# First layer in 512-token tiles for the last 1536 tokens, with a new opening list: a fused attention and two-MLP kernel

## The chip, the cores and the metric

One core of a Trainium2 chip runs the whole kernel. The metric is the device time of one execution in microseconds (us); three runs give a median. TensorE does the matmuls, VectorE (DVE in the rows), ScalarE (ACT) and GpSimd (POOL) the elementwise work, and SyncE (SP) issues most transfers.

## The reference

A banded attention (each token sees the 64 tokens up to itself) over 4 sequences of 576 tokens, 8 heads of 64, then two MLPs, the first with a leaky Relu whose slope is given by column, the second with x times sigmoid(x):

```python
scores = scale * np.matmul(q, k.transpose(0, 1, 3, 2))
mask = (rel >= 0) & (rel < window)              # rel = row - column, window = 64
scores = np.where(mask, scores, -1000000000.0)
attn = np.exp(scores - np.max(scores, axis=-1, keepdims=True))
attn = attn / (np.sum(attn, axis=-1, keepdims=True) + 1e-09)
x = np.matmul(attn, v)                          # laid out as 2304 tokens x 512
...
h = x @ w_in                                    # 512 -> 2048
g = np.maximum(h, 0.0) + alpha * np.minimum(h, 0.0)
x = g @ w_out                                   # 2048 -> 512
...
h = x @ w_in2
out = (h * (1.0 / (1.0 + np.exp(-h)))) @ w_out2
```

All is float32. Where more precision than one pass is wanted the kernel writes a number as a high and a low part and adds three products (high by high, high by low, low by high).

## The kernel before, in words

The 2304 tokens lie in six tiles of 384 (`TN`). An **item** is one tile and one pair of heads, so there are 24; items 0 to 3 make tile 0. An item goes through scores (`mm_s`, S in the list, line 220), the row maximum (`peaks`, m, L231, VectorE), the exponential (`exps`, e, L243, ScalarE), the sum's reciprocal (`over`, r), the scaling (`scaled`, s: on GpSimd with P, on ScalarE with A at L267, else on VectorE), transposes (`mm_t`, t, L278), a copy out of PSUM (`keep_t`, k, L287), the product with v (`mm_v`, P, L300), and the split of the result into a high part (`high_v`, x, L310, ScalarE) and a low part (`low_v`, l, L316, VectorE). m, e, r, s, t and k go by halves a and b.

The first layer's product `mlp_h1` (M, L400) takes, for one tile and one of 16 blocks of 128 columns (f), 4 x 3 matmuls into a bank h. `fall_g1` (G, L406, ScalarE) and `join_g1` (J, L415, VectorE) make the leaky Relu, and `store_g1` (L428) writes it to device memory.

The program has these stages. **The opening**: a list written out by hand, `START`, gives the order of items 0 to 11, of the scores and softmax of 12 and 13, of the conversion of the 16 weight blocks (c, h, o), and of all first-layer work of tiles 0 and 1. **The rest of the first layer**: a loop over tiles 2 to 5 and f, 64 steps; every eighth step begins a group with two more items (`begin`), and a plan of numbered places (`hook`) puts the conversion of later weights between the steps. **The first layer's second product** (L496): 3 x 56 steps of Strassen-like sums with parts named A11, A21, A22, A12; `load_g1` (L445) fetches the Relu's results, `sum_g1` (L453) adds, `split_g1` splits into high and low parts (L346, L347), three steps ahead of their use. Then the second MLP (L575, L695 and L699).

Small tiles have fixed places: `room(i)` in one pool, `wroom(i)` in another, both by hand. Each engine works through its own queue in order; a wait holds all behind it.

Of the kernel before, what the change touches and what calls it, by code (L numbers as in the profile page):

```python
# [20 lines left out]
q0 q2 S0 S2 m0a q3 S3 m0b m2a z m2b q1 e0a e0b e2a r0b S1 v0 q5 q4 e2b r0aP s0aP r2a m3a m3b r2b m1a t0a m1b s2aP e3a  # L21
e3b t2a r3aP S5 k2aD k0aD s2bP e1a e1b s0bP s3aP S4 m5a e5a m5b r1aP r3bP q7 r1bP t2b q6 v1 v2 q8 m4a t0b k2bD S7 S6
s1aP s1bP k0bD e4a m7a t1a e5b t3a t1b s3bP m4b r5aP m6a r4aP t3b r5bP m6b e4b P0 s5aP k3b P2 k1aD k1bD s5bP t5a e6a
k3aD t5b r4bP m7b P1 e6b k5aD s4aP s4bP P3 x2 r6b t4b e7a l2 t4a S8 v5 v6 r6aP v4 w1 k5bD s6bP k4bD r7aP t6b k4a m8a
e7b x0 x3 m8b r7b s6aP q9 q11 P4 P5 k6b s7aP s7bP q10 t6a c1a l0 l3 t7a e8a k7a c1b t7b x1 w6 S9 k7bD k6a P7 P6 x4 c1c
h1 x7 l1 x5 e8b r8aP m9a m9b s8aP e9a l7 w7 S11 S10 o1 l5 l4 r8b t8a s8bA M0.1.1 M1.1.3 c6a m10a M0.1.2 r9aP x6 v8 v9
M0.1.3 M1.1.0 e9b t8b k8b c6b s9aP w2 M1.1.1 k8aD l6 w3 q13 r9b c6c M0.1.0 m10b P8 c7a h6 c7b e10a t9a s9bP v10 t9b
k9b o6D m11a k9a M1.1.2 M0.6.1 M1.6.0 c7c m11b e11a G1.1 c2a h7 c3a x8 M0.6.2 M0.6.0 r10aP c3b r11a l8 e10b M1.6.2 c2b
e11b o7D M1.6.1 M1.6.3 r11b s10aP c3c P9 G0.1 w8 w5 q12 x9 t10a M0.6.3 M1.7.2 M0.7.0 k10a M0.7.2 G1.6 h3 l9 r10bP
M1.7.3 M1.7.1 M0.7.3 c2c v11 s11aA J0.1 J1.1 G0.6 s10bA M1.7.0 s11bA J1.6 J0.6 o3 M0.7.1 t10b t11a t11b c8a k10b c8b  # L30
P10 c5a c5b k11a k11b S12 S13 c5c c8c h5 m12a G1.7 P11 M1.3.2 h8 m13a h2 o5 m12b m13b x11 J1.7 o2D w10 w4 w9 x10 c10a
o8 l11 c10b M0.5.3 M1.3.3 M0.8.3 M1.8.2 M1.2.0 l10 c4a c10c M1.2.2 M0.2.1 c4b M1.3.0 c4c M1.2.3 G0.7 M1.5.0 h10 M1.5.3
M1.8.1 M1.5.1 h4 w11 o10D o4 M1.5.2 M1.3.1 M0.8.2 M1.2.1 c11a c11b G1.5 G1.3 c11c c9a M0.2.2 M0.8.1 M1.8.0 J1.3 J1.5
h11 M0.8.0 w12 w0 w13 c9b M1.10.1 c12a c0a c9c M0.10.1 M0.2.3 G1.2 G0.8 c12b M1.10.3 M1.10.0 M0.5.0 J0.8 c12c M0.5.2
M0.2.0 G0.2 M0.4.1 M0.4.2 M0.10.2 h9 c0b M1.10.2 J0.7 J0.2 o11D o9 h12 M0.5.1 M0.11.0 M0.11.2 w14 v12 v13 w15 e12a
J1.2 o12 c13a M0.11.1 e12b M1.12.1 M0.4.0 c14a M0.4.3 c0c M0.3.3 M1.8.3 c13b M0.11.3 c13c M1.12.2 c15a M1.12.3 G0.5
M0.10.3 G0.4 G1.8 G0.11 J0.5 M1.9.0 c15b c15c M1.9.3 M0.10.0 M1.9.1 M0.3.2 h15 J0.4 G0.10 M1.11.3 M1.11.1 J1.8 J0.10
M1.9.2 G1.9 M0.12.0 h0 h13 M1.4.0 M0.12.1 c14b M1.12.0 o15D o0D M0.3.0 M1.11.2 M1.4.2 M0.3.1 M0.12.3 c14c M1.11.0 o13
J1.9 M0.15.0 h14 M0.12.2 J0.11 G1.12 J1.12 o14 r12a M0.15.1 G0.3 M0.0.3 J0.3 G1.10 M1.14.0 M0.0.1 M1.14.3 M0.0.0
M0.15.2 e13a G1.11 M0.15.3 M1.14.2 M0.9.3 J1.10 M1.14.1 M1.13.2 J1.11 M1.4.1 M1.0.1 G0.12 G0.15 M1.13.3 M1.13.1 J0.12  # L40
M0.14.1 M1.0.2 e13b M0.14.0 M0.9.1 M1.13.0 s12aP r13bP M0.0.2 M1.4.3 G0.0 r13a r12bP M1.0.3 M0.14.3 M1.0.0 J0.15 G1.4
M0.9.0 M0.9.2 M0.14.2 M0.13.1 G1.14 G1.13 s13bA s12bA J1.13 M0.13.3 G1.0 G0.14 G0.9 M0.13.0 M0.13.2 J0.9 J1.4 J1.14
G0.13 M1.15.3 J0.0 J0.14 M1.15.1 J0.13 M1.15.0 J1.0 M1.15.2 s13aP G1.15 J1.15
# [8 lines left out]
def attention_two_mlps(ctx, tc, q, k, v, w_in1, w_out1, alpha, w_in2, w_out2, out):  # L52
# [7 lines left out]
    TN = 384  # L60
    NTILE = NT // TN
# [24 lines left out]

    def room(i, shape=None, dtype=F32, name="r"):
        return rp.tile(shape or [P, TN], dtype, name=name, tag=f"r{i}")

# [50 lines left out]
    AHEAD = 3 * NHP  # L140
    spare = {"pr": [*range(28, 34), 36, 37], "pt": [38, 39, 34, 35], "bank": list(range(8))}
# [4 lines left out]
    def give(kind, i, n=0):  # L146

        if kind == "pt" and i < 36 and n == NHP + 3:
            kind = "pr"
        if kind != "pr" or i > 33 or n < NHP:  # L150
            spare[kind].append(i)
# [11 lines left out]
    def load_qk(n):  # L163
# [5 lines left out]
        queue = nc.scalar if len(items) < 3 else nc.sync  # L169
        items.setdefault(n, {}).update(qT=qt, kT=kt)  # L170
        if n == 0:
# [132 lines left out]

    def high_v(n):
        t, hp = divmod(n, NHP)

        at = 2 * hp + (32 if t == 2 else 8 * (t % 2))
        xh, xl = (wroom(at + i, [P, TN], F32R, "x") if t == 2 else room(at + i, None, F32R, "x") for i in range(2))
        nc.scalar.copy(xh, items[n]["pv"][:, :TN])  # L310
        xt[t, hp] = (xh, xl)

    def low_v(n):
        it = items.pop(n)
        xh, xl = xt[divmod(n, NHP)]
        nc.vector.tensor_tensor(out=xl, in0=it["pv"][:, :TN], in1=xh.bitcast(F32), op=ALU.subtract)  # L316
        give("bank", it["pvi"])
        if n >= AHEAD:
            load_v(n + 2)
# [67 lines left out]
    gd1 = {}  # L387
    turn_g = Turn(range(16, 28))
# [14 lines left out]
    def fall_g1(t, f):  # L403

        a = room(turn_g(), name="a")
# [5 lines left out]
    def join_g1(t, f):  # L411
# [6 lines left out]
        store_g1(3)  # L418
# [4 lines left out]
    def store_g1(keep):  # L423

        while len(unstored) > keep:
            t, f, g = unstored.pop(0)
            d = gd1[t, f] = dram.tile([P, TN], F32, name=f"g1_{t}_{f}")
# [383 lines left out]
    for w in START.split():  # L811
# [15 lines left out]
        else:  # L827
            n = int(w.rstrip("abADP"))
# [8 lines left out]
            elif x == "r":  # L837
                over(n, (hf,), engine)
# [168 lines left out]
    g = -62  # L1007
    for x in "0 1 a 2 3 b 4 5 c 6 7 d e".split():
# [36 lines left out]
    spare["pt"] += [26, 27]  # L1045
# [27 lines left out]
    for t in range(2, NTILE):  # L1073
        for f in range(KF):
            rests()
            s = (t - 2) * KF + f
            if s in group:
                begin(s, group[s])
            for x in soft.pop(s, ()):
                x()  # L1080
            mlp_h1(t, f, at=(turn_h5 if t == NTILE - 1 else turn_h)())
            fall_g1(t, f)
            if last:
                join_g1(*last)
            last = t, f
            hook((t - NTILE) * KF + f)
            if t == NTILE - 1:
                if f == 0:
                    nc.scalar.activation(out=silu_tables, in_=ident[:, :1], func=AF.Silu)
                if 4 <= f < 4 + KH:  # L1090
                    load_g1(0, A11, f - 4)
                if 8 <= f < 12:
                    load_g1(0, A21, f - 8)
                if f >= KF - 3:
                    split_g1(f - KF + 3)
# [102 lines left out]
```

## Time and profile before

| | |
|---|---|
| median of three runs | 796.95 us (796.12 to 797.12) |
| the profiled execution's own time | 795.78 us |
| its span | 794.0 us |
| TensorE busy | 784.9 us, 99% of the span |
| VectorE busy | 634.8 us, 80% |
| ScalarE busy | 491.7 us, 62% |
| GpSimd busy | 122.4 us, 15% |

The span is what the profiler saw of the program; the execution's own time holds 1.8 us more. Matmuls are pipelined, so two that follow each other overlap in the rows, and the distance of their starts is the cost of one.

### The profile page before, as it was taken

What the parts mean: (1) busy time and instruction counts of PE and PEld (TensorE: products, weight loads), DVE (VectorE), ACT (ScalarE), POOL (GpSimd) and SP (SyncE); (2) the same over time, 40 slices, a digit from 0 to 9 for tenths busy, and PEclk for the clock granted to TensorE, in tenths of its full rate; (3) what the DMA queues carried; (4) which work ended last, traced back from release to release, by engine and by line L of the source; (5) the groups of instructions that cost most, each with busy time, mean ns of one, the idle gap of its engine ahead of it and who ended that gap; (6) DMA issues with size and microseconds to landing.
All of it is one profiled execution on the core that took longest, in us unless ns stands there. A gap on an engine that the chain in (4) does not pass through costs nothing.

```text
span 794.0 us, 16666 instructions
## 1 busy us (share of the span) xinstructions
PE 784.9 (99%) x5475; PEld 754.0 (95%) x5475; DVE 634.8 (80%) x1613; ACT 491.7 (62%) x1312; POOL 122.4 (15%) x160
## 2 busy tenths in 40 slices
PE   7999999999999999999999999999999999999998
PEld 5899999999999999999999999999999888888887
DVE  6999457888888998978889775765985988868876
ACT  7974366677633675564587566545766675555553
POOL 6522200000000132231222000000000331321410
PEclk9999999999999999999999999999999999999999
DMA  9978376888595879998987765795758997958922
GB/s 298 313 254 279 124 234 219 283 258 297 186 308 207 280 154 260 285 229 237 291 238 202 241 210 184 243 335 181 247 179 274 298 263 219 209 129 235 204 50 72
DMA packets 126151, 182.79 MB, mean 230 GB/s; under 512 B 12976, under 2 KB 112048, under 8 KB 126064
## 3 DMA queue, kind: packets, MB, share of 16 engines
q1 hardware_dynamic: 111664, 162.25, 61.5%
q0 software_dynamic: 13824, 18.88, 14.5%
q8 instruction: 43, 0.70, 0.4%
q10 hardware_dynamic: 576, 0.59, 0.2%
q14 instruction: 44, 0.36, 0.1%
HBM read 105.52 MB, written 57.28 MB: 205 GB/s over the span
## 4 chain that ended last, share of the span: by engine, by line
PE 96%; ACT 1%; DVE 1%; DMA 1%; issue 0%; POOL 0%; ACTq 0%; POOLq 0%
PE h L400 25%; PE acc L496 22%; PE acc L695 15%; PE qa L575 13%; PE acc L699 7%; PE qd L575 6%; PE qb L575 3%; PE pa L300 2%; PE pa L220 2%; PE pa L278 1%; ACT pr L243 1%; DVE pr L231 1%; DMA kT<-in_k_dram 1%; PE acc L691 0%; ACT x L310 0%
## 5 line engine op out<-in xcount | busy, mean ns | idle before, releaser
L400 PE MATMUL h<-x,i 128*128 128x384 f32 x1152 | 203.1, 335 | 0.1
L400 PEld LDWEIGHTS h<-x,i 128*128 128x128 f32 x1152 | 199.0, 188 | 1.3 <-DVE i L372 0.4
L695 PE MATMUL acc<-w,gh 128*128 128x512 f32 x489 | 169.2, 394 | 0.0
L496 PE MATMUL acc<-gh,o 128*128 128x384 f32 x672 | 143.5, 334 | 0.0
L699 PE MATMUL acc<-w,gl 128*128 128x256 f32 x489 | 134.3, 277 | 0.0
L346 ACT CAST gh<-gf 128x384 fp32r<-128x384 f32 x168 | 86.2, 515 | 58.8 <-PE acc L496 52.7
L496 PEld LDWEIGHTS acc<-gh,o 128*128 128x128 f32 x672 | 118.9, 188 | 0.0
L695 PEld LDWEIGHTS acc<-w,gh 128*128 128x128 f32 x489 | 91.1, 188 | 20.6
L575 PE MATMUL qa<-v,w 128*128 128x384 f32 x576 | 107.9, 334 | 0.0
L347 DVE TENSOR_TENSOR gl<-gf,gh 128x384 fp32r<-128x384 f32 x168 | 91.5, 551 | 18.6 <-ACT gh L346 13.6
L575 PEld LDWEIGHTS qa<-v,w 128*128 128x128 f32 x576 | 100.6, 188 | 0.0
L346 ACT CAST gh<-g 128x384 fp32r<-128x384 f32 x124 | 63.6, 514 | 54.6 <-PE acc L695 48.7
L699 PEld LDWEIGHTS acc<-w,gl 128*128 128x128 f32 x489 | 91.8, 188 | 0.8
L406 ACT ACTIVATE a<-h 128x384 f32<-128x384 f32 x96 | 46.1, 489 | 72.0 <-PE h L400 69.8
L455 POOL DMA_DIRECT2D gf<-gf x48 | 42.6, 941 | 287.5 <-DVE gf L453 208.0
L496 PE MATMUL acc<-gl,o 128*128 128x384 f32 x336 | 85.2, 334 | 0.0
L347 DVE TENSOR_TENSOR gl<-g,gh 128x384 fp32r<-128x384 f32 x124 | 67.0, 552 | 13.7 <-ACT gh L346 13.3
L654 POOL DMA_DIRECT2D g<-g x40 | 34.8, 879 | 278.6 <-ACT gh L346 195.6
L415 DVE SCALAR_TENSOR_TENSOR a<-a,nalpha,h 128x384 f32<-128x384 f32 x96 | 57.0, 606 | 12.5 <-ACT a L406 12.4
L243 ACT ACTIVATE pr<-pr,nm 128x128 f32<-128x128 f32 x144 | 56.1, 394 | 10.5 <-DVE nm L231 10.4
L496 PEld LDWEIGHTS acc<-gl,o 128*128 128x128 f32 x336 | 60.7, 188 | 0.0
L575 PE MATMUL qd<-v,w 128*128 128x384 f32 x288 | 57.6, 334 | 0.0
(103 smaller groups left out, 1114.3 us busy)
## 6 DMA issues: line engine op xcount, KB each, us to landing
g<-a SPq DMA_DIRECT2D x96, 192.0 KB, 4.1
gf<-g SPq DMA_DIRECT2D x96, 192.0 KB, 4.1
g<-c SPq DMA_DIRECT2D x96, 192.0 KB, 3.3
g<-g SPq DMA_DIRECT2D x96, 192.0 KB, 4.2
s<-in_moe_w_in_dram SPq DMA_DIRECT2D x32, 512.0 KB, 5.7
s<-in_moe_w_out_dram SPq DMA_DIRECT2D x32, 512.0 KB, 5.3
gf<-gf POOLq DMA_DIRECT2D x48, 192.0 KB, 5.1
g<-g POOLq DMA_DIRECT2D x40, 192.0 KB, 4.2
```

The source lines that it names most:

```text
L243: nc.scalar.activation(out=pr[:, j, :], in_=pr[:, j, :], func=AF.Exp, bias=it[f"nm{hf}"][:, j:j + 1], scale=-1.0, accum_out=it["sm"][:, hf ...
L346: nc.scalar.copy(hi, src)
L347: lows.append(lambda: nc.vector.tensor_tensor(out=lo, in0=src, in1=hi.bitcast(F32), op=ALU.subtract))
L400: nc.tensor.matmul(h, w[:, kk, :], x, start=not done and n == 0, stop=len(done) == KD - 1 and n == 2)
L406: nc.scalar.activation(out=a, in_=begun[t, f][1], func=AF.Relu, scale=-1.0)
L415: nc.vector.scalar_tensor_tensor(out=a, in0=a, scalar=nalpha[:, f:f + 1], in1=h, op0=ALU.mult, op1=ALU.add)
L455: nc.gpsimd.dma_start(out=o, in_=g1[u, b, c], accum_op=ALU.add)
L496: nc.tensor.matmul(o[i], w[:, a, i * P:(i + 1) * P], b, start=start and a == 0 and b is gh, stop=c == KH - 1 and b is gl, skip_group_check ...
L575: nc.tensor.matmul(o, w[:, a, k0], b, start=start and kk == 0 and n == 0, stop=kk == 1 and n == 2, skip_group_check=True)
L654: nc.gpsimd.dma_start(out=gb[u, a, c], in_=gb[u, b, c], accum_op=ALU.add)
L695: nc.tensor.matmul(acc2[u, v][i], gh[:, i * P:(i + 1) * P], w.rearrange("p a d -> p (a d)"), start=first, stop=final, skip_group_check=True)
L699: nc.tensor.matmul(acc2[u, v][i][:, :HD], gl[:, i * P:(i + 1) * P], w[:, 0, :], start=False, stop=final, skip_group_check=True)
```

## The change

The last 1536 tokens go through the first layer in three tiles of 512 (`LN`) instead of four of 384; the first 768 stay in two tiles of 384. The loop has 48 steps instead of 64, and the same 64 plan places are spread over them. An item's result now falls into one or two wide tiles (`spans`). Four items more (12 to 15), and the scores and softmax of 16 and 17 instead of 12 and 13, go into the opening, whose list is written anew, so that four groups are left (every seventh step) instead of six. The first two k loads instead of the first three go on ScalarE's queue. Rooms 8 to 23 become a pool that is closed and opened anew twice, at the opening's end and at the first layer's end; the Relu's results of the wide tiles have four rooms (before, ten), one of them unstored at a time (before, three), and go into one memory tile per f. A11's first four parts, instead of three, are split ahead of the second product.

```diff
+    LN = 512
...
-    AHEAD = 3 * NHP
-    spare = {"pr": [*range(28, 34), 36, 37], "pt": [38, 39, 34, 35], "bank": list(range(8))}
+    AHEAD = 4 * NHP
+    spare = {"pr": [*range(28, 34), 36, 37], "pt": [38, 39, 34, 35, 26, 27], "bank": list(range(8))}
...
-        queue = nc.scalar if len(items) < 3 else nc.sync
+        first, queue = not items, nc.scalar if len(items) < 2 else nc.sync
...
+    def turn_pool(name):
+        if few:
+            few["in"].__exit__(None, None, None)
+        few["in"] = tc.tile_pool(name=name, bufs=1)
+        few["pool"] = few["in"].__enter__()
...
+    def spans(t, hp):
+
+        if t < 2:
+            if (t, hp) not in xt:
+                xt[t, hp] = tuple(room(16 + 2 * hp - 8 * t + i, None, F32R, "x") for i in range(2))
+            return [(xt[t, hp], slice(0, TN), slice(0, TN))]
+        at, end, found = (t - 2) * TN, (t - 1) * TN, []
+        for u in range(at // LN, (end - 1) // LN + 1):
+            if (u, hp) not in xw:
+                xw[u, hp] = tuple(wide_x(u, hp, i) for i in range(2))
+            a, b = max(at, u * LN), min(end, (u + 1) * LN)
+            found.append((xw[u, hp], slice(a - u * LN, b - u * LN), slice(a - at, b - at)))
+        return found
...
-            begun[t, f] = at, bank(at, "h")[:, :TN], []
+            begun[t, f] = at, bank(at, "h")[:, :TN if t < 2 else LN], []
...
-            xh, xl = xt[t, kk]
+            xh, xl = xt[t, kk] if t < 2 else xw[t - 2, kk]
...
-        store_g1(3)
+        store_g1(3 if t < 2 else 1)
...
-    turn_g.rooms, turn_g.n = list(range(16, 26)), 8
+    turn_g.rooms, turn_g.n = [8, 9, 10, 11], 0
...
-    group = {8 * i: AHEAD + 2 * i for i in range((NI - AHEAD) // 2)}
+    group = {7 * i: AHEAD + 2 * i for i in range((NI - AHEAD) // 2)}
...
+    turn_pool("rb")
+    steps = 3 * KF
+    for s in range(steps):
+        t, f = 2 + s // KF, s % KF
...
+        for g in range(-FIRST * s // steps, -FIRST * (s + 1) // steps):
+            hook(FIRST + g)
...
+            if f >= KF - 4:
+                split_g1(f - KF + 4)
...
+    turn_pool("rc")
     for n in range(NU * STEPS):
         rests()
         around1(n)
-        split_g1(n + 3)
+        if n:
+            split_g1(n + 3)
```

ScalarE's queue in the opening, around the first scaling that ScalarE does (item 8's second half; `pr` are the probabilities, `pt` the transposed ones, `x` an item's high part). Before:

```order
L243 ACTIVATE pr,sm<-pr,nm 128x128 [waits Pool_49]
L243 ACTIVATE pr,sm<-pr,nm 128x128 x2
L243 ACTIVATE pr,sm<-pr,nm 128x128 [waits DVE_49,Activation_49]
L243 ACTIVATE pr,sm<-pr,nm 128x128 [waits DVE_49] x2
L267 ACTIVATE pr<-pr,rs 128x128 [waits DVE_49,Activation_49]
L267 ACTIVATE pr<-pr,rs 128x128 [waits Activation_49] x2
L310 CAST x<-pa 128x384 [waits PE_49]
```

and in the change:

```order
L261 ACTIVATE pr,sm<-pr,nm 128x128 [waits DVE_49] x3
L261 ACTIVATE pr,sm<-pr,nm 128x128 [waits Pool_49]
L261 ACTIVATE pr,sm<-pr,nm 128x128 x2
L305 COPY pt<-pa 128x384 [waits PE_49,Activation_49]
L285 ACTIVATE pr<-pr,rs 128x128 [waits DVE_49]
L285 ACTIVATE pr<-pr,rs 128x128 [waits Activation_49] x2
L442 ACTIVATE a<-h 128x384 [waits PE_49]
```

Before, an item's high part followed the scaling; now the first Relu of an h bank does.

ScalarE's queue behind a group's transposes, in the first step of the loop. Before:

```order
L310 CAST x_1942<-pa_1929 128x384 [waits PE_49]
L310 CAST x_1963<-pa_1950 128x384 [waits PE_49]
L406 ACTIVATE a_1984<-h_1971 128x384 [waits DMAHW7_49,PE_49]
```

and in the change:

```order
L347 CAST x_1566<-pa_2228 128x256 [waits PE_49]
L347 CAST x_2241<-pa_2228 128x128
L347 CAST x_1577<-pa_2251 128x256 [waits PE_49]
L347 CAST x_2264<-pa_2251 128x128
L442 ACTIVATE x_2287<-h_2274 128x512 [waits PE_49]
```

The high parts of these two items go out in two pieces, and the Relu has 512 columns.

SyncE's queue at the end of the first layer: the last stores of the Relu's results, and the first loads of A21's parts 4 to 7 (`gf`). Before:

```order
L428 DMA g_5_14_4209<-a 128x384 [waits DMAHW2_49,DVE_49]
L428 DMA g_5_15_4211<-a 128x384 [waits DMAHW3_49,DVE_49]
L445 DMA gf<-g_1_4_1834 128x384 [waits DMAHW4_49,PE_49,Activation_49]
L445 DMA gf<-g_1_5_1434 128x384 [waits DMAHW5_49]
```

and in the change:

```order
L471 DMA g_14_3008<-x 128x512 [waits DMAHW2_49,DVE_49]
L471 DMA g_15_3039<-x 128x512 [waits DMAHW3_49,DVE_49]
L488 DMA gf<-g_1_4_2140 128x384 [waits DMAHW3_49,DMAHW4_49,DMAHW2_49,DMAHW6_49,DMAHW1_49,DMAHW7_49,DMAHW0_49,Activation_49]
L488 DMA gf<-g_1_5_2161 128x384 [waits DMAHW5_49]
```

The first load waited for one transfer queue and two engines; now it waits for all the transfer queues, on which the last stores lie.

## Rows read from the trace of the kernel before

**Rows 1.** The page: busy us, share of the span and instructions of each engine.

```profile
PE 784.9 (99%) x5475; PEld 754.0 (95%) x5475; DVE 634.8 (80%) x1613; ACT 491.7 (62%) x1312; POOL 122.4 (15%) x160
```

**Rows 2.** The chain of waits in order of time: start us, us, what.

```profile
52.71 54.48 PE h L400 x312
107.19 1.31 PE pa L278 x12
108.50 1.47 PE pa L220 x48
109.97 1.55 PE pa L300 x48
111.52 16.85 PE h L400 x96
...
216.02 50.12 PE h L400 x288
266.15 174.72 PE acc L496 x1008
```

**Rows 3.** Timeline of TensorE in the last product: start us, us, instructions.

```profile
715.17 0.63 PE L695 MATMUL acc<-w,gh 128*128 128x512 f32 x2
715.64 0.28 PE L699 MATMUL acc<-w,gl 128*128 128x256 f32 x1
...
731.84 0.62 PE L695 MATMUL acc<-w,gh 128*128 128x512 f32 x2
732.30 0.28 PE L699 MATMUL acc<-w,gl 128*128 128x256 f32 x1
...
789.38 0.40 PE L691 MATMUL acc<-w,gh 128*128 128x256 f32 x2
789.62 0.28 PE L691 MATMUL acc<-w,gl 128*128 128x256 f32 x1
```

**Rows 4.** Windows: us, busy (count) by engine, clock, DMA share, GB/s.

```profile
20.00:40.00 20.00, 19.92 (x339) 17.58 (x335) 19.62 (x90) 19.45 (x82) 11.26 (x17) 1.00 0.91 309
...
80.00:100.00 20.00, 20.00 (x117) 20.00 (x116) 9.26 (x19) 7.39 (x24) 4.72 (x6) 1.00 0.32 112
...
151.00:172.00 21.00, 21.00 (x208) 20.56 (x200) 17.69 (x59) 15.25 (x55) 0.00 (x0) 1.00 0.90 295
```

The engines stand in the order PE, PEld, DVE, ACT, POOL.

**Rows 5.** Timeline of TensorE: the first h matmuls.

```profile
32.12 2.86 PE L400 MATMUL h<-x,i 128*128 128x384 f32 x15
```

**Rows 6.** Timeline of ScalarE in the opening.

```profile
5.45 0.40 ACT L243 ACTIVATE pr<-pr,nm 128x128 f32<-128x128 f32 x1 [1.55 <-DVE nm L231]
...
6.24 0.39 ACT L243 ACTIVATE pr<-pr,nm 128x128 f32<-128x128 f32 x1
...
19.62 0.45 ACT L287 COPY pt<-pa 128x384 f32<-128x384 f32 x1
19.98 0.40 ACT L243 ACTIVATE pr<-pr,nm 128x128 f32<-128x128 f32 x1
```

**Rows 7.** Timeline of SyncE's queue at the first layer's end.

```profile
267.35 0.32 SPq L428 DMA_DIRECT2D g<-a  x1
267.77 0.86 SPq L445 DMA_DIRECT2D gf<-g  x2
```

**Rows 8.** Transfers issued then: count, KB each, median us to landing.

```profile
gf<-g SPq DMA_DIRECT2D x2, 192.0 KB, 3.5
g<-a SPq DMA_DIRECT2D x1, 192.0 KB, 1.9
```

**Rows 9.** From 108 us on: landings of the Relu's stores, SyncE's longest wait.

```profile
DMA to landing us min/median/max: 1.8/4.7/7.5
...
SPq L202 <- PE pa L300: 24.2, 5, 8.5
```

The second row gives the total, the times and the longest.

**Rows 10.** Timeline of VectorE early in the second product.

```profile
274.21 0.54 DVE L453 TENSOR_TENSOR gf<-gf 128x384 f32<-128x384 f32 x1
...
282.25 0.54 DVE L347 TENSOR_TENSOR gl<-gf,gh 128x384 fp32r<-128x384 f32 x1
```

More of the change, by code (lines that the diff above doesn't have):

```diff
@@ L26 @@
[L26 to L35, printed above, removed]
@@ L146, in give @@
     def give(kind, i, n=0):
-        if kind == "pt" and i < 36 and n == NHP + 3:
+        if kind == "pt" and i in (34, 35) and n >= NHP + 3:
             kind = "pr"
@@ L303, in mm_v, with wide_x @@
             give("pt", it[f"pti{hf}"], n)
-    def high_v(n):
[L306 to L311, printed above, removed]
+    xw = {}
+    def wide_x(u, hp, i):
+        if u == 2:
+            return broom(2 * hp + i, F32R)
+        return wroom(52 + hp + 8 * i if u else 32 + 2 * hp + i, [P, LN], F32R, "x")
+    def spans(t, hp):
[10 more added lines that the diff above has]
+        return found
+    def high_v(n):
+        for (xh, _), to, c in spans(*divmod(n, NHP)):
+            nc.scalar.copy(xh[:, to], items[n]["pv"][:, c])
     def low_v(n):
         it = items.pop(n)
-        xh, xl = xt[divmod(n, NHP)]
-        nc.vector.tensor_tensor(out=xl, in0=it["pv"][:, :TN], in1=xh.bitcast(F32), op=ALU.subtract)
+        for (xh, xl), to, c in spans(*divmod(n, NHP)):
+            nc.vector.tensor_tensor(out=xl[:, to], in0=it["pv"][:, c], in1=xh[:, to].bitcast(F32), op=ALU.subtract)
         give("bank", it["pvi"])
@@ L385, in combos @@
             sub(t[:, 3, :], b21, t[:, 1, :], ALU.add if minus else ALU.subtract)
-    gd1 = {}
-    turn_g = Turn(range(16, 28))
+    gd1, gw1 = {}, {}
+    turn_g = Turn((*range(8), 24, 25))
     turn_h, turn_h5 = Turn((0, 1, 2)), Turn((4, 6, 2))
@@ L403, in fall_g1 @@
     def fall_g1(t, f):
-        a = room(turn_g(), name="a")
+        a = room(turn_g(), name="a") if t < 2 else broom(turn_g(), F32)
         nc.scalar.activation(out=a, in_=begun[t, f][1], func=AF.Relu, scale=-1.0)
@@ L426, in store_g1 @@
             t, f, g = unstored.pop(0)
-            d = gd1[t, f] = dram.tile([P, TN], F32, name=f"g1_{t}_{f}")
+            if t < 2:
+                d = gd1[t, f] = dram.tile([P, TN], F32, name=f"g1_{t}_{f}")
+            else:
+                if t == 2:
+                    gw1[f] = dram.tile([P, NT - 2 * TN], F32, name=f"g1_{f}")
+                    for x in range(2, NTILE):
+                        gd1[x, f] = gw1[f][:, (x - 2) * TN:(x - 1) * TN]
+                d = gw1[f][:, (t - 2) * LN:(t - 1) * LN]
             nc.sync.dma_start(out=d, in_=g)
@@ L837, in attention_two_mlps @@
             elif x == "r":
-                over(n, (hf,), engine)
+                over(n, (0, 1) if w.rstrip("P").endswith("c") else (hf,), engine)
             elif x == "t":
@@ L1005, in LEFT @@
         return [slot(u, c, h) for c, h in ((5, 5), (6, 0), (6, 1), (6, 3), (6, 5), (7, 2), (7, 3), (7, 4), (7, 5), (8, 0), (8, 6))]
-    g = -62
-    for x in "0 1 a 2 3 b 4 5 c 6 7 d e".split():
+    g = -63
+    for x in "0 1 a 2 3 b c d e 4 5 6 7".split():
         if x.isdigit():
@@ L1072, in attention_two_mlps @@
     store_g1(0)
[L1073 to L1095, printed above, removed]
+    turn_pool("rb")
+    steps = 3 * KF
+    for s in range(steps):
+        t, f = 2 + s // KF, s % KF
+        rests()
+        if s in group:
+            begin(s, group[s])
+        for x in soft.pop(s, ()):
+            x()
+        mlp_h1(t, f, at=(turn_h5 if t == 4 else turn_h)())
+        fall_g1(t, f)
+        if last:
+            join_g1(*last)
+        last = t, f
+        for g in range(-FIRST * s // steps, -FIRST * (s + 1) // steps):
+            hook(FIRST + g)
+        if t == 4:
+            if f == 0:
+                nc.scalar.activation(out=silu_tables, in_=ident[:, :1], func=AF.Silu)
+            if 4 <= f < 4 + KH:
+                load_g1(0, A11, f - 4)
+            if 8 <= f < 12:
+                load_g1(0, A21, f - 8)
+            if f >= KF - 4:
+                split_g1(f - KF + 4)
     join_g1(*last)
     store_g1(0)
+    turn_pool("rc")
     for n in range(NU * STEPS):
```

51 lines of the change are left out of this document (34 added, 17 removed).

## The prediction

> **What bounds the kernel now.** I read the page first, for the share of each engine. TensorE is busy 99% of the span [rows 1], so only two things can shorten the run: fewer or cheaper matmuls, or less time in which TensorE cannot start one. The chain of waits in order of time tells where it runs without a gap [rows 2]: from 52.71 us to the end of the first stage at 266.15 us every piece is a TensorE piece, and the second product goes on from there. The time that is not full lies before 52.71 us. To size it I count TensorE's work in the opening by the chain's own rows: a pair of items takes 1.31 us of transposes, 1.47 of scores and 1.55 of values, so one item 0.655, 0.735 and 0.775, and an h matmul of 384 columns 50.12/288 = 0.1740 us [rows 2]. The opening of before holds 14 score sets, 12 transposes, 12 value sets and 384 h matmuls: 10.3 + 7.9 + 9.3 + 66.8 = 94.3 us. It ends at 107.19, so 12.9 us are lost in it. At the first h matmul, 32.12 us [rows 5], 12 score sets, 17 half transposes and 8 value sets had been done, 20.6 us: 11.5 of the 12.9 are lost by then. What TensorE waits for there is the softmax of the first eight items: between 20 and 40 us ScalarE is busy 19.45 and VectorE 19.62 of 20 us, and at 80 to 100 us both are more than half free [rows 4].
>
> **The widened first layer.** 768 matmuls of 384 columns become 576 of 512, the same 294,912 columns. The trace of before has no 512-column h matmul, but the last product has 512- and 256-column ones. Start to start, two 512s in a row take 0.46 us in one place and 0.47 in another (six such pairs stand in the trace, all 0.46 or 0.47), so 0.232 each; two 256s in a row take 0.24, so 0.120 [rows 3]. Against 0.1740 for 384 the 512 is 4/3 as dear (0.1740 x 4/3 = 0.232): by this row width saves nothing, 768 x 0.1740 = 133.6 us against 576 x 0.232 = 133.6. The other bound comes from the 256s: a line through 0.120 and 0.1740 has 0.422 ns a column and 12 ns a matmul, and would put a 512 at 0.228, 131.3 us in all, 2.3 us less. I take the first, since it is the operation itself, and keep 0 to -2.3. The Trainium skill, "TensorE: Matmul & The Clock Gate", section "Wait — 56ns, not 53.3ns?", gives a back-to-back matmul at full clock as its columns over 2.4 GHz plus about 2.5 ns; by that the 768 would take 124.8 us and the 576 124.3, a gain of 0.5. The trace has 174 and 232 ns where the page has 162.5 and 215.8, so the rows decide.
>
> The 64 steps of this part become 48, and its groups of attention work six become four, since four items more lie in the opening. Their transposes, scores and values cost the same in both places, and TensorE bounds both: 0. A block of 96 matmuls behind a group takes 16.85 us where 96 x 0.1740 is 16.70 [rows 2]; two such places fewer give -0.3.
>
> Wider Relus and joins, and the copies of an item's values in two pieces where it straddles two wide tiles, fall on ScalarE and VectorE, which are busy 15.25 and 17.69 of 21 us there [rows 4] while a group's distance grows from 16.7 + 4.3 to about 7 x 2.78 + 4.3 = 23.8 us: hidden. The planned conversions run 4 for each 3 steps, so at the old pace in time.
>
> The intermediate tiles now have four rooms instead of ten. A step's room is wanted again four steps later, 4 x 2.78 = 11.1 us, and its join ends some 1.5 us after its matmuls; 9.6 us are left for the issue and the landing, which took 4.7 us in the median and 7.5 at most [rows 9]. SyncE has been held up to 8.5 us at the value loads [rows 9], but such a hold ends inside the next group, at its value matmuls, and the group puts 4.3 us more between a step and its successor four on; the last join ahead of a group then waits some 4 us, and 10 lie open even so. Cost 0. Were that cover gone, ScalarE would stand in the Relu, and behind it the copies of the weights' highs; TensorE would feel it only after its three banks of h are used up.
>
> **The opening list.** It holds 18 score sets, 16 transposes, 16 value sets and the same 384 h matmuls: 13.2 + 10.5 + 12.4 + 66.8 = 102.9 us. What matters is the time lost with it. The exponentials begin at 5.45 us, set by VectorE, which waits for the scores and these for k; three take 3 x 0.39, and the 384-column copies 0.36 start to start [rows 6]. I follow item 8's second half, whose scaling ScalarE does: in the old order it stood ahead of the first h matmul's Relu with few copies before it, now the first Relu stands directly behind it. Ahead of its transposes TensorE has, by the new list, 11 score sets, 17 halves, 8 value sets and 30 h matmuls, 8.1 + 5.6 + 6.2 + 5.2 = 25.1 us; ScalarE has 20 halves of exponentials and some 21 smaller instructions, 20 x 1.17 + 21 x 0.36 = 31.0 us, so 5.45 + 31.0 = 36.4 at the earliest, and 11.3 us are lost there at the least, without any slip. So the start is no better fed than before (11.5 at the first h matmul). Behind it the new list asks less: before lost 12.9 - 11.5 = 1.4 us more between the first h matmul and the end. I take the same loss as before, 0, and keep -1.5 (nothing is lost after the first fork) to +1.4 (that loss once more, with 8 halves of exponentials more to carry). The four items' softmax is hidden late in the opening, where VectorE is busy 9.26 and ScalarE 7.39 of 20 us [rows 4]; were it early, it would cost 4 x 2 x 1.17 = 9.4 us of ScalarE.
>
> The k load that leaves ScalarE's queue saves it one issue ahead of the table load; the first exponential waited 1.55 us for VectorE anyway [rows 6]: 0. It stands eighth among the first loads, and item 0's softmax is third in line, 4.7 us after 5.45: hidden.
>
> **The turn into the second product.** The split of A11 one step ahead takes one low part of 0.54 us [rows 10] off VectorE there: 0, because TensorE does not wait there now. But four loads (A21, parts 4 to 7) go into rooms that now belong to a pool closed and opened anew, and by the order the first of them waits for every transfer queue, so for the landing of the last store of the first layer; behind it in SyncE's queue stand the eight A22 loads. Before, the last store was issued at 267.35 and the first load at 267.77 [rows 7], 1.6 us after 266.15, without waiting for it. Now, by the wider Relu and join (from 128x256 to 128x384 a VectorE or ScalarE row grows by some 0.12 us, an estimate), the last store goes out about 1.45 us after the turn; at the 1.9 us that the last store took to land, or 2.5 for a third more bytes, and 3.5 for the load [rows 8], the data are there 6.9 to 7.5 us after the turn. The sum that reads them runs at 274.21, 8.06 after it [rows 10]: 0. If the store lands later, VectorE stands at that sum with the low parts queued behind it, which TensorE needs: that of step 16 was done at 282.8 and wanted at 266.15 + 16 x 1.04 + 0.70 = 283.5, 0.7 us to spare [rows 10].
>
> **The sum.** 0 (columns) - 0.3 (groups) + 0 (opening) + 0 (turn) = -0.3 us. On the profiled execution's own 795.78 us (span 794.0) that is 795.5; the median of the three runs, 796.95, lies 1.17 above it, so 796.7.
>
> **The rivals.** *A matmul has a fixed price*, the 2.3 us above: for it, the step from 256 to 384 columns costs close to one column at 2.4 GHz each; against it, both pairs of 512s. With the -0.3 it gives 794.4. *The opening packs better*: what before lost behind the first h matmul is not lost again, -1.5 - 0.3, so 795.2; for it, the new list puts the later conversions and joins further back; against it, ScalarE's 11.3 us at item 8. *The reload waits*, the one that ends slower: the last store lands as slowly as the layer's others do, 4.7 to 7.5 us. TensorE loses time once it takes over 8.06 + 0.7 - 1.45 - 3.5 = 3.8 us; at 4.7 it costs 0.9, at 7.5 3.7, in the middle 2.3: 796.95 - 0.3 + 2.3 = 799.0. Against it, the last stores before landed in 1.9, with little other traffic. That the change does not do what it says is excluded: the order shows the 512-column matmuls.
>
> **How the numbers follow.** About 1.6 us, 0.2%, is what a measurement here can tell from no change. I give the forecast 0.55 (its own range 795.4 to 798.2), the fixed price 0.15, the better opening 0.12, the slow reload 0.18. All of the forecast is within 0.2%; the second and third are faster, the fourth slower. The range 793.8 to 799.1 takes in the first three and the smaller half of the fourth's price, and leaves out the two faster ones together, and the full price of the reload.
>
> **What would show it.** In the changed profile: 512-column h matmuls 0.232 us apart (0.228 or less would show the fixed price); the last h matmul of the opening ending at 102.9 + 12.9 = 115.8 us; the second product starting near 115.8 + 133.6 + 4 x 2.86 + 3 x 1.47 + 4 x 0.15 = 265.8 (eight items and three pairs of scores are left); VectorE's fifth sum of the second product without a wait for a transfer. An opening that loses under 11.5 or over 14 us, or TensorE standing between 274 and 284 us, makes the prediction wrong.

## The result, and the profile after

The changed kernel takes 803.37 us (median of 4 runs, 801.72 to 805.13) against 796.99 of the kernel before: a ratio of 1.0083, 95% interval 1.006 to 1.0105. It is slower by 6.4 us, where 796.7 and "no change" were forecast. The profiled execution took 805.13 us, the longest of the four; its span is 803.3. Two executions of later sets, 2760.15 us with all pools 128 bytes higher and 2005.34 us in the yardstick of the fourth set, were in a slow state and weigh nothing in the intervals.

The page of the changed kernel (share of engines; then the group of first-layer matmuls: busy us, mean ns of one, idle time ahead):

```profile
span 803.3 us, 16187 instructions
...
PE 789.7 (98%) x5283; PEld 734.7 (91%) x5283; DVE 632.2 (79%) x1601; ACT 483.1 (60%) x1281; POOL 124.9 (16%) x163
...
L436 PE MATMUL h<-x,i 128*128 128x512 f32 (+1 forms) x960 | 202.1, 371 | 0.0
```

TensorE is busy for 789.7 us, 4.8 more than before [rows 1], for the same columns in 192 matmuls fewer. So not only waits were added: the same work takes longer. The chain of waits of the changed kernel (start us, us, what) says where:

```profile
75.88 20.74 PE h L436 x117
...
119.58 1.31 PE pa L296 x12
...
151.09 0.61 ACT x L442
...
151.72 0.75 DVE x L451
...
154.87 6.95 DMA g<-x
...
161.84 0.64 SPq L364
...
162.52 7.98 DMA g<-x
...
170.58 0.60 ACT x L442
171.18 0.38 ACT pt L305
...
171.60 2.18 PE pa L238 x44
173.79 2.55 PE pa L318 x48
...
198.62 74.96 PE h L436 x324
273.57 175.26 PE acc L539 x1008
```

| stage ends at, us | forecast | measured | over |
|---|---|---|---|
| opening | 115.8 | 119.58 | 3.8 |
| first layer (second product starts) | 265.8 | 273.57 | 4.0 more |
| span | 793.7 | 803.3 | 1.8 more |

Three things stand in these rows that the forecast did not have. First, 117 matmuls of 384 columns take 20.74 us, 0.1773 each, where before had 0.1740 [rows 2]. Second, between 151 and 171 us the chain leaves TensorE and runs through two stores of Relu results (`g<-x`, 6.95 and 7.98 us from issue to landing), a Relu (L442) and a copy for the values (L305). Third, the scores and values behind that stand are slow, 2.18 us for 44 matmuls and 2.55 for 48 where a pair of items takes 1.47 and 1.55 [rows 2]. The stretches say why (PE busy and count, PEld, DVE, ACT, POOL, the granted clock, DMA share, GB/s):

```profile
168.80:171.60 2.80, 0.25 (x4) 0.01 (x1) 0.29 (x1) 1.02 (x3) 0.00 (x0) 1.00 1.00 362
171.60:176.20 4.60, 4.60 (x92) 4.14 (x92) 1.10 (x7) 2.81 (x10) 0.00 (x0) 0.63 0.17 64
176.30:181.00 4.70, 4.70 (x23) 3.89 (x22) 4.18 (x9) 1.08 (x2) 0.00 (x0) 1.00 0.87 274
```

TensorE stood for 2.6 us, and then had a mean granted clock of 0.63 over 4.6 us: (1 - 0.63) / 0.5 x 4.6 = 3.4 us of them at 1.2 GHz in place of 2.4, 1.7 us lost. In a second profile of the same kernel (the first run below) it stood for 1.3 us at the same place and the clock stayed at 1.00:

```profile
170.01 1.22 PE L238 MATMUL pa<-kT,qT 64*64 64x128 f32 x32 [1.33 <-ACT pt L305]
...
170.00:174.00 4.00, 3.99 (x96) 3.50 (x97) 1.53 (x8) 3.30 (x11) 0.00 (x0) 1.00 0.37 140
```

In the opening TensorE waits for these (line, releaser: us, times, longest):

```profile
PE pa L238 <- DMA kT<-in_k_dram: 4.8, 2, 3.4
PE pa L318 <- issue: 1.3, 1, 1.3
PE pa L296 <- POOL pr L287: 0.9, 2, 0.5
PE pa L238 <- issue: 0.7, 1, 0.7
```

The two "issue" waits have no releaser in the profile, and no waits of that kind stand in the opening of before. The timeline shows them in the middle of runs of like instructions:

```profile
25.33 0.29 PE L318 MATMUL pa<-pt,vo 128*64 128x64 f32 x4
26.95 0.28 PE L318 MATMUL pa<-pt,ve 128*64 128x64 f32 x3 [1.33 <-issue]
...
31.86 0.44 PE L238 MATMUL pa<-kT,qT 64*64 64x128 f32 x5
32.99 1.52 PE L238 MATMUL pa<-kT,qT 64*64 64x128 f32 x43 [0.70 <-issue]
```

Counted over matmuls and weight loads, the first stands behind TensorE's 705th instruction and the second behind its 961st, 256 apart. The record of transfers shows one of 16 KB on the instruction queue at 24.6 to 25.6 us and one at 30.8 to 31.7; both stands end 1.3 us after such a transfer. The pages list these transfers, in the changed kernel and in the kernel before:

```profile
q8 instruction: 41, 0.67, 0.3%
```

```profile
q8 instruction: 43, 0.70, 0.4%
```

That is 16 KB each, and two fewer for the 384 matmuls and weight loads that the changed kernel saves. In the kernel before the same counts, 705 and 961, are passed at 23.7 and 29.4 us, behind transfers that ended at 22.2 and 27.4, and TensorE does not stand there.

So there were three theories: *places* (where a streamed tile lies sets a matmul's price), *rooms* (four rooms are too few for stores that land late), *code* (TensorE waits for its next 256 instructions; the first expectation calls it *opening*). All times below are medians; each set has its own runs of the kernel before, 796.57 to 796.85. The interval in brackets is that of the ratio to it.

### The profile page after: what moved, and what is told of

Read it like the earlier page. It is cut to its first block, busy times and chain, and to the rows that moved or that the text cites. A ratio compares the mean times of both kernels' runs of the same rounds, so it can differ in the third digit from the quotient of the medians.

```text
span 803.3 us, 16187 instructions
## 1 busy us (share of the span) xinstructions
PE 789.7 (98%) x5283; PEld 734.7 (91%) x5283; DVE 632.2 (79%) x1601; ACT 483.1 (60%) x1281; POOL 124.9 (16%) x163
## 4 chain that ended last, share of the span: by engine, by line
PE 95%; DMA 2%; ACT 1%; DVE 1%; issue 0%; POOL 0%; ACTq 0%; SPq 0%
PE h L436 23%; PE acc L539 22%; PE acc L738 14%; PE qa L618 13%; PE acc L742 7%; PE qd L618 6%; PE qb L618 3%; PE pa L318 2%; PE pa L238 2%; DMA g<-x 2%; PE pa L296 2%; ACT pr L261 1%; DMA kT<-in_k_dram 1%; POOL pr L287 0%; ACT x L442 0%
## 5 line engine op out<-in xcount | busy, mean ns | idle before, releaser
L436 PE MATMUL h<-x,i 128*128 128x512 f32 (+1 forms) x960 | 202.1, 371 | 0.0
L436 PEld LDWEIGHTS h<-x,i 128*128 128x128 f32 x960 | 174.9, 188 | 24.1
L442 ACT ACTIVATE x<-h 128x512 f32<-128x512 f32 x48 | 28.6, 596 | 69.1 <-PE h L436 62.0
L618 PEld LDWEIGHTS qd<-v,w 128*128 128x128 f32 x288 | 50.9, 188 | 0.0
```

The source lines that it names most:

```text
L436: nc.tensor.matmul(h, w[:, kk, :], x, start=not done and n == 0, stop=len(done) == KD - 1 and n == 2)
L442: nc.scalar.activation(out=a, in_=begun[t, f][1], func=AF.Relu, scale=-1.0)
L618: nc.tensor.matmul(o, w[:, a, k0], b, start=start and kk == 0 and n == 0, stop=kk == 1 and n == 2, skip_group_check=True)
```

## The experiments

### First set: places and rooms

**The changed kernel again.** 

> The changed kernel once more, unchanged, as the yardstick of this set and as a second trace of it. Theory 'places' (the streamed operand of a matmul costs TensorE more when its tile lies high in the partition) expects the same slow matmul spacings at the same tiles: 384 columns 175 to 177 ns in the opening and in part of the product behind 448 us, 512 columns 227 ns up to the third wide tile and 230 to 237 in it, some 3.8 us in all. Theory 'rooms' (a Relu waits until the store of the step four earlier has landed) expects TensorE to stand once or more between 120 and 200 us, by an amount that differs from run to run. Theory 'opening' expects the two stalls of TensorE without a named cause (1.33 and 0.70 us, 256 instructions apart) near 25 and 32 us. If the slow spacings were chance, they would be gone or elsewhere. Time 801.5 to 805.

Measured: 802.29 us (ratio 1.0067, 1.0052 to 1.0081). The slow spacings came at the same matmuls, the two stands in the opening (1.1 and 0.9 us) behind the same instructions, and the store wait was shorter. So the spacing belongs to the program and the store wait's size to the run.

**Small pools at the upper end.**

```diff
-    stg = ctx.enter_context(tc.tile_pool(name="stg", bufs=4))
+    stg = ctx.enter_context(tc.tile_pool(name="stg", bufs=4, side="right"))
```

and the same for `cv`, `tp`, `kp` and `sml`. 

> The changed kernel with its five small pools moved to the upper end of the partition, so that the pool of the first layer's tokens, Relu results and the later products' rooms lies at 170784 to 195360 bytes of a partition in place of 203424 to 228000; no instruction and no wait changes. Theory 'places' expects every 384-column matmul back at 173.3 ns and every 512-column one at 226.7, 3.8 us less: 799.6. A rival, that the slow spacing comes from the stalls ahead of it (the engine falls into another rhythm after a wait), expects no change, 803.4, and slow spacings at the same times. What the rooms and the opening cost stays in both.

Measured: 799.51 us (1.0015 to 1.0038), 2.8 less than the changed kernel in this set. The chain in the opening and across the second and third wide tiles:

```profile
77.84 17.34 PE h L436 x100
...
223.85 38.31 PE h L436 x169
```

That is 173.4 and 226.7 ns a matmul, as where no tile had moved; the rival, a rhythm after a stall, falls.

**The kernel before with its rooms opened last.** The line of the pool `rp` moves behind that of `sml`. 

> The kernel before with one line moved: the pool of its 384-column rooms is opened last and so lies at 166560 to 228000 bytes in place of 133920 to 195360; 1200 of its 3168 matmuls of 384 columns then stream a tile from above 196608 bytes. Theory 'places' expects 1200 x 2.4 ns = 2.9 us more, 799.9 (a little more or less if the border lies elsewhere), and matmuls of 175 to 177 ns at those tiles alone. The rival (a rhythm after a stall) expects no change, 797.0.

Measured: 805.76 us (1.0097 to 1.0123), 9.1 us more. The sign is right, the size is not, and neither is the theory: tiles at 168 KB are slow here, which were fast at the same height in the kernel before. One stretch of the opening's first-layer matmuls in the chain of before, then of this run:

```profile
59.83 35.21 PE h L400 x203
```

```profile
59.91 35.20 PE h L400 x200
```

173.4 against 176.0 ns a matmul. What the slow cases have in common is where their tiles start in a partition, as the built program places them: 203424 and 166560 are 160 past a multiple of 256, while the fast 133920, 170784 and the weights' 2848 are 32 past one. Tiles are multiples of 256 long, so all of a pool share this. The 9.1 us lie in all three products that stream 384 columns and in the last one.

**Stores on GpSimd's queue.**

```diff
-        store_g1(3 if t < 2 else 1)
+        store_g1(3 if t < 2 else 0)
...
-            nc.sync.dma_start(out=d, in_=g)
+            (nc.gpsimd if t >= 2 else nc.sync).dma_start(out=d, in_=g)
```

> The changed kernel with the 48 stores of wide Relu results issued by GpSimd, each right behind its join, in place of SyncE one join later; GpSimd has no work between 120 and 270 us, and SyncE stands for up to 7.3 us at value loads there. Theory 'rooms' expects no Relu to wait for a store any more and TensorE not to stand between 120 and 200 us: 4.3 us less than the profiled execution (2.6 us of standing and 1.7 us at the lower clock behind it), some 3 less in the median: 800.4. A rival, that the landing itself is what is long (7 to 8 us when the queues are full) and the queue of issue does not matter, expects the same waits and 803.4. The slow matmul spacings stay in both.

Measured: 800.21 us (1.0026 to 1.0051), 2.1 less than the changed kernel in this set. No Relu waits for a store, and TensorE does not stand between 120 and 270 us.

### Second set: height or offset

**128 bytes ahead of the rooms' pool.**

```diff
+    gap = ctx.enter_context(tc.tile_pool(name="gap", bufs=1))
+    nc.vector.memset(gap.tile([P, 32], F32, name="gap"), 0.0)
     turn_pool("ra")
```

> The changed kernel with 128 unused bytes a partition ahead of the pool of the first layer's rooms, which then starts at 203552 in place of 203424, still the highest of all; one small memset is added. Theory 'height' (tiles above some 166 to 196 KB are slow to stream) expects nothing: 802.3, spacings of 175 to 177 and 230 to 237 ns where they were. Theory 'offset' (a streamed tile that starts 160 bytes past a multiple of 256, as at 203424 and 166560, is slower than one 32 bytes past it, as at 133920 and 170784) expects 173.3 and 226.7 ns everywhere and 3.8 us less: 798.5.

Measured: 798.47 us (1.0014 to 1.0037), as *offset* (where within 256 bytes a tile starts) has it; *height* (how far up it lies) falls. The chain of the changed kernel, in the opening, in the first wide tiles and in the third one (each the one piece of its window):

```profile
77.83 17.20 PE h L436 x98
...
199.97 26.09 PE h L436 x115
...
228.78 33.36 PE h L436 x143
```

and of the one with 128 bytes more:

```profile
76.85 18.20 PE h L438 x105
...
228.82 33.32 PE h L438 x147
```

In ns a matmul: 175.5, 226.9 and 233.3, against 173.3 and 226.7. The first two wide tiles are in the pool of the weights, the third in the moved pool, as is the opening's.

**All pools 128 and 224 bytes higher, in the kernel before.** The same two lines (32 and 56 columns) ahead of the pool `wp`. 

> The kernel before with 128 unused bytes ahead of all its large pools: weights and streamed tiles both start 160 bytes past a multiple of 256 in place of 32. If the start of the streamed tile alone decides, all 3168 matmuls of 384 columns take 2.6 ns more, 8.2 us, and the last product's something too: 805 to 807. If what counts is that weights and streamed tile start differently (the weight load runs beside the stream), nothing changes: 796.6. Theory 'height' expects nothing either.

> The kernel before with 224 unused bytes ahead of all its large pools, so that weights and streamed tiles start on a multiple of 256. If only the difference between the two counts: no change, 796.6. If the streamed tile's own start counts, this says whether a start on the multiple is as good as 32 past it (796.6) or the 173.3 ns of a 384-column matmul still hold some nanoseconds that a better start gives back (each ns would be worth 3.2 us).

Measured: 796.81 (0.9994 to 1.0012) and 796.60 us (0.9993 to 1.001): nothing. So it is not the streamed tile's own start that counts, but whether it and the operand that TensorE loads as its weights start alike within 256 bytes.

**64 bytes between weights and rooms, in the kernel before** (run in the third set). The two lines, 16 columns, ahead of `rp`. 

> The kernel before with 64 unused bytes between the pool of weights and the pool of its 384-column rooms, so that streamed tiles of the rooms start 64 bytes off the weights' place within 256 bytes, where the run with the rooms opened last had 128 off and 9.1 us more. If any difference costs the same: 805.8. If only 128 of 256 is bad: 796.6. In between: a price that grows with the difference.

Measured: 799.54 us (1.0023 to 1.0046), 2.7 more. Neither expectation: the 384-column matmuls keep their 173.3 ns, and only the last product pays, which alternates 512 and 256 columns. A stretch of 120 us of it, before and then here (matmuls of each kind):

```profile
L695 PE MATMUL acc<-w,gh 128*128 128x512 f32 x347 | 120.0, 394 | 0.0
```

```profile
L697 PE MATMUL acc<-w,gh 128*128 128x512 f32 x341 | 120.0, 397 | 0.0
```

and in the kernel with its rooms opened last:

```profile
L695 PE MATMUL acc<-w,gh 128*128 128x512 f32 x343 | 120.0, 393 | 0.0
```

So in this product 64 bytes cost more than 128. It differs from the others in two ways: by its two shapes, and by its roles, for here the tokens' tiles from the rooms are loaded as weights and the weight matrix is streamed. Which of the two makes it pay at 64 bytes was not run.

**Both mended**: the 128 bytes and GpSimd's stores. 

> The changed kernel with the 128 unused bytes and with GpSimd issuing the 48 wide stores right behind their joins. If the two losses are apart, their gains add: 802.3 - 3.8 (spacings, as in the run with the pools moved) - 2.1 (the store wait, as measured with GpSimd alone) = 796.4, as fast as before; what is left over the predicted 796.7 less the cheaper wide matmuls would be the opening's. If spacings and waits share a cause, less: 798 or more.

Measured: 796.37 us (0.9991 to 1.0009), and 796.62 (0.9991 to 1.0017) in a later set. The two losses are apart and add up.

### Third set: the opening, and what made the stores late

**32 small matmuls first.**

```diff
+    spin = bank(spare["bank"][-1], "pa")
+    for _ in range(32):
+        nc.tensor.matmul(spin[:W, :W], ident[:, :W], ident[:, :W], start=True, stop=True)
     for w in START.split():
```

> The version with the 128 bytes and GpSimd's stores, with 32 small matmuls of no use (64 instructions, counting weight loads) at the very start, where TensorE waits for the first tokens. In all five profiles of the changed kernel and its variants so far TensorE stands without a named cause behind its 705th and its 961st instruction, 256 apart, for 1.0 to 1.8 and 0.7 to 1.4 us, whatever it computes there, and some 1.3 us behind a transfer of 16 KB on the instruction queue. Theory 'code' (TensorE waits for its next 256 instructions, whose transfer stands behind the opening's loads) expects the stands again at a count of 705 and 961, so 64 instructions earlier in the work, with a sum of 0 to 3 us. A rival, that a certain matmul of the list waits for something that the trace does not name, expects them at 769 and 1025. Time 796.4, or up to 2 less where the earlier border is met in time.

Measured: 798.24 us (1.001 to 1.0029). Both stands were gone, which neither *code* nor its rival had expected. But the matmuls lasted until 6.8 us and held up the first scores, so the time says nothing of the price; and they were 128 instructions, not 64, since the trace has each of them twice, with a weight load each time.

**A weight load 4 us later.** In the opening list `w7` goes from behind `w6` to behind `q11`. 

> The version with the 128 bytes and GpSimd's stores, with one 512 KB load of weights (the second one of the opening) issued some 4 us later, behind two more loads of queries and keys. Theory 'code' expects the first of the two transfers of instructions to come 1 to 1.5 us sooner (512 KB at 350 GB/s are 1.5 us), and TensorE's stand behind instruction 705 to shrink from 1.8 to 0 to 0.8 us, while the second may grow; 796.4 - 1 = 795.4 at the best, 796.4 at the worst. If the stands have nothing to do with the loads, nothing changes.

Measured: 797.54 us (0.9995 to 1.0016). The transfer ahead of the first stand starts at 24.0 us, where it started at 24.1 in the version that this one is built on, and not 1 to 1.5 us sooner; the stands last 1.3 and 0.4 us. There is no gain, and since the transfer did not move, the trial speaks neither for *code* nor against it.

**The store one join earlier, still on SyncE.** Only the first line of the diff of GpSimd's stores. 

> The changed kernel with one number changed: a wide store is issued by SyncE right behind its own join and not behind the next one. Theory 'rooms' with the queue as its cause (SyncE stands at value loads with the stores behind them) expects part of what GpSimd's queue gave, 0.5 to 1.5 of 2.1 us: 801 to 802. If the one join of delay is the whole cause, 800.2 as with GpSimd. If it is the landing alone, 802.3.

Measured: 799.67 us (1.0022 to 1.0046), the same as with GpSimd within the intervals. What ScalarE waits for ahead of the wide Relus (us, times), in the changed kernel:

```profile
  PE h L436: 62.0, 39
  DMA g<-x: 4.6, 2
```

and here, where the wait for a store is gone:

```profile
  PE h L436: 64.7, 41
```

So taking away the one join of delay is enough. GpSimd's queue with the delay kept was not run.

### Fourth and fifth set: what the code stands cost

**The yardstick.** 

> The version with the 128 bytes and GpSimd's stores once more, as the yardstick of this set: 796.4 (its first set) to 797.5 (the version with one load later, which changed nothing in the trace beyond 0.3 us). TensorE stands behind its instructions 705 and 961 for 2 to 2.8 us together, and the opening's last first-layer matmul ends near 118.4.

Its result is told above; its opening ends at 117.7 us in the profile (by TensorE's timeline, which has such ends 0.16 us earlier than the chain).

**32 matmuls in the form of the scores**, 64 rows by 64 by 128 columns on the corners of two banks. 

> The same with 32 matmuls of no use in the form of the scores (64x64, 64 rows by 128 columns; 128 instructions with their second passes and weight loads) ahead of the first scores. They should end by 3.4 us, when the first keys land, where the earlier trial took until 6.8 and so delayed the first softmax by some 2.5 us. Theory 'code' expects no stand at 705 and 961 (as in the earlier trial, where the border fell into thinner work), the opening to end 2 us sooner, near 116.2, and 794.4. A rival, that the first items' softmax on VectorE and ScalarE sets the opening's end and the stands lie beside it, expects the stands gone, waits for scaled halves in their place, an end near 118 and 796.4.

Measured: 796.75 us (0.9994 to 1.0012), no gain over 796.62, while the profile's opening ends at 117.0. The stands are gone; TensorE's waits up to 36 us are now

```profile
PE pa L298 <- POOL pr L289: 2.6, 2, 2.2
PE pa L859 <- POOL ident masks.py:199: 1.4, 1, 1.4
PE pa L240 <- DMA kT<-in_k_dram: 0.5, 2, 0.3
PE pa L298 <- DVE sm L279: 0.3, 1, 0.3
```

**The same with SyncE's early stores.** 

> The changed kernel with the 128 bytes, the same 32 matmuls, and the wide stores issued by SyncE behind their own joins in place of GpSimd. By the run with that edit alone (2.6 us less than the changed kernel's own 802.3) SyncE does as well as GpSimd: the same time as the run with GpSimd and the 32 matmuls, within 0.5 us. If SyncE's stand at value loads matters after all, TensorE stands again between 120 and 200 us and it is 1 to 2 us slower.

Measured: 795.28 us (0.9976 to 0.9994). Unlike forecast it is 1.5 us faster than with GpSimd's stores.

**Without the 32 matmuls, and with them again.** 

> The changed kernel with the 128 bytes and the wide stores issued by SyncE behind their own joins, without the 32 matmuls of no use. Against the same with them (795.3): if TensorE's stands behind instructions 705 and 961 cost what the openings' ends say (117.7 to 118.5 without, 116.4 to 117.0 with the 32 matmuls), it is 1 to 1.5 us slower, 796.3 to 796.8. If the stands lie beside the softmax, 795.3; the 1.4 us between the two versions with the 32 matmuls would then be GpSimd's queue alone.

> The same with the 32 matmuls again, on the same chip and in the same set: 795.3, against 796.6 of the kernel before; its stands at 705 and 961 stay gone, and TensorE waits some 2 us for scaled halves near 10 us in their place.

Measured: 796.34 us (0.9987 to 1.0005) without, 795.59 (0.9975 to 0.9993) with. The intervals overlap a little. With SyncE's stores the 32 matmuls gain 0.8 us here, 1.1 against the set before, and with GpSimd's stores nothing (796.62 and 796.75), of the 1.6 to 2.4 that the two stands last together. With them TensorE waits once for 1.9 to 3.5 us for scaled halves near 11 us, and behind that wait its granted clock falls, in all four profiles with the 32 matmuls; without them it does not. The same stretch without and with (columns as above):

```profile
13.50:17.00 3.50, 2.25 (x43) 1.69 (x36) 3.50 (x28) 3.50 (x19) 3.25 (x6) 1.00 1.05 369
```

```profile
13.50:17.00 3.50, 3.46 (x52) 2.73 (x43) 3.50 (x28) 3.50 (x19) 3.34 (x6) 0.53 0.99 328
```

That is (1 - 0.53) / 0.5 x 3.5 = 3.3 us at 1.2 GHz, some 1.6 us of TensorE's work lost, in a stretch in which it would in part have waited anyway. So the gain of the 32 matmuls is not the price of the stands, which these runs do not give by itself. They do settle what the stands are. In the last profile one of 0.3 us is left:

```profile
22.95 0.28 PE L320 MATMUL pa<-pt,ve 128*64 128x64 f32 x3
23.58 0.22 PE L320 MATMUL pa<-pt,ve 128*64 128x64 f32 x1 [0.34 <-issue]
```

It lies behind the 705th instruction again, 128 instructions earlier in the work than before, and ends 1.3 us behind a transfer of 16 KB that ended at 22.3. That is as *code* has it; the rival, a certain matmul that waits for something unnamed, falls. This version, the changed kernel with 128 bytes, one number and 32 matmuls of no use, is the only one that is faster than the kernel before: by 0.15% in both sets, and than the changed one by 0.8 to 1%.

## Why the prediction was wrong

**The steps that failed** are three terms of the sum that stand there at 0: the price of a matmul's place, the four rooms, and the opening.

The first is "768 matmuls of 384 columns become 576 of 512, the same 294,912 columns", priced at what such matmuls take in the kernel before. The change also moves the rooms of the first layer's tokens into a pool that it opens last, and so 128 bytes off the weights within 256. That part was not costed at all. Summed over the distances of the trace, against those of the version with 128 bytes more, it costs 0.8 us in the opening, 1.3 in the third wide tile and 1.4 behind the second product, 3.5 together. In the medians, taking it away gave 2.8 us within one set (802.29 to 799.51, the pools moved) and 3.8 across two (802.29 to 798.47, the 128 bytes).

**Four rooms, "Cost 0"**, failed too. The 9.6 us were counted from the join to the landing, but a store is issued only behind the next join, one step of 2.7 us later, and then behind queries, keys and weights in SyncE's queue; and the two landings in the chain took 6.95 and 7.98 us where the median had been 4.7 and the longest 7.5 [rows 9]. The order of consequences was as written: the Relu stands, behind it ScalarE's copies. But TensorE felt it through the copy for the values (L305) behind the Relu, not through banks of h. It cost 4.3 us in the profiled run, with the lower clock, and 2.1 in the medians (798.47 to 796.37).

**The opening, "the same loss as before, 0"**, was 3.8 us off: 115.8 forecast, 119.58 measured. It lost 16.7 us, more than the 14 that the prediction named as a sign of being wrong. 0.8 of the 3.8 is the spacing and 2.0 are the two code stands of this profile, though taking such stands away gave back 1.1 us of the median at the most; the rest, 1.0, has no named cause. The floor from ScalarE at item 8 was not refuted: when the code stands went, a longer wait for the softmax and the lower clock behind it took part of their place. The rival of an opening that packs better fell with this.

**The fixed price per matmul**, a rival at 0.15, was right in its mechanism. 384 columns take 173.3 ns and 512 take 226.7 at 2.4 GHz: 32 columns' time, 13.3 ns, on top of the columns. 768 x 173.3 - 576 x 226.7 = 2.5 us gained, against the 2.3 of that rival. The forecast read its rows rightly: a 512 of the last product takes 0.232 us. But there it stands among matmuls of another shape and with the roles told above, and its price did not carry over to long runs of nothing but 512s, which the trace of before does not have. The Trainium skill, "TensorE: Matmul & The Clock Gate", section "Wait — 56ns, not 53.3ns?", has a fixed price too, of about 2.5 ns; the distances here show 13.3, and they decide.

**The reload that waits**, the slow rival at 0.18, did not come about: the sums of the second product wait for no transfer, and TensorE does not stand from 273.57 to 290 us. So the one rival that forecast a slower kernel was right in the sign by luck: its reason did not come about.

**The groups** (-0.3) and **the split of A11** (0) can't be told apart in size: the version without spacing and store waits takes 148.2 us from the end of the opening to the second product, and the forecast's 150.05 less 3.0 for the cheaper 512s (576 x 0.0053) makes 147.0. Of the 1.2 us more, 0.6 lie in the first group's scores, which take 2.1 us behind a copy of ScalarE where 1.47 were counted, and the rest in the borders between shapes. The k load shows nothing either way.

All together, in the profiled run: 3.5 (spacing) + 4.3 (stores and clock) + 3.0 (opening without spacing) + 1.2 (group and borders) + 0.5 (the second product, 175.26 us against 174.72 [rows 2], and 175.26 with the 128 bytes too; its cause is open) - 3.0 (512s below 0.232) = 9.5 of the 9.6 us over the forecast span. That the version with both losses mended takes 796.4, next to the forecast 796.7, is luck: there the cheaper 512s make good what the opening loses.

## What to carry to other kernels

When a change opens, closes or reorders pools, compare where weights and streamed tiles start within 256 bytes, and compare the distance of like matmuls in a stretch without waits: 1 to 3% there leaves the busy share of TensorE as it was (99% in the kernel before, and with its rooms opened last), and here was some 3 us. Count a room's round from its writing to the landing with every delay the code itself puts ahead of the store, and against the longest landing under load, not the median. A stand without a releaser, a fixed number of instructions from the next one, may be a wait for code: look for a transfer on the instruction queue ahead of its end. Taking it away gains only what the next wait, and the clock behind that wait, leave.

## What the runs showed of the hardware

- A 384-column matmul whose streamed tile starts 128 bytes off its weights within 256 takes 175.5 to 176 ns in place of 173.3, a 512-column one 233.3 in place of 226.7. At 64 bytes off, 384 columns were not slower, but the last product was, with its 512 and 256 columns and the tokens as loaded weights: 341 pairs in 120 us in place of 347, some 3 us in all. Shifting both by 128 or 224 changes nothing. That TensorE's weight load and its stream meet in the same part of the memory would fit; it was not shown. The Trainium skill, "SBUF — State Buffer", section "SBUF: two separate sides", says that TensorE's port never waits on anyone. No run here shows another engine to blame, so it may be TensorE's own two reads that meet.
- The granted clock fell behind a stand of 2.6 us and not behind one of 1.3 at the same place; 3.4 us at 1.2 GHz cost 1.7, two thirds of the stand itself. It fell as well behind the wait of 1.9 to 3.5 us near 11 us in the four profiles with the 32 matmuls.
- TensorE's code came in pieces of 256 instructions (16 KB). In the opening, with the transfer engines 88% taken over the first 40 us, a piece came so late that TensorE stood for 0.4 to 1.6 us at the borders 705 and 961 in all ten profiles of the changed kernel and its versions without the extra matmuls; with 128 instructions put first, the borders fell elsewhere in the work, and of four profiles one has a stand there, of 0.3 us.
- Stores of 256 KB issued by GpSimd landed in time, yet with the 32 matmuls the same kernel was 1.5 us slower with them than with SyncE's (796.75 and 795.28, the profiled executions 0.6 apart); without the 32 matmuls there was no difference (796.62 and 796.34, in two sets). Why is open.
